# A fused attention, gated-MLP and residual kernel: LayerNorm of chunk 1 brought forward, its loads and spreads put in another order

## The chip, the core and the metric

The kernel runs on one core of one Trainium2 chip. The metric is the device time of one execution in microseconds (us); it is given as the median of several executions. The profile is of one further execution. Its span runs from its first to its last instruction and is a little shorter than that execution's device time.

## What is computed

One transformer block without the second normalization: x is normalized over its 640 columns (2048 rows, bfloat16), and both a sliding-window attention (32 heads of 20, window 256) and a gated MLP (640 to 1536 to 640) read the normalized rows. Both results are added to x.

```python
xn = _layernorm(x, axis=-1)
return x + _A_ref(xn, A_wqkv, A_wo) + _B_ref(xn, B_w_gate, B_w_up, B_w_down)

# _A_ref
qkv = (x @ wqkv).reshape(B, S, 3, H, Dh).transpose(2, 0, 3, 1, 4)
scores = einsum("bhqd,bhkd->bhqk", q, k) * (Dh ** -0.5)
scores = where(mask, scores, -1e9)      # 0 <= i - j < 256
o = einsum("bhqk,bhkd->bhqd", softmax(scores), v)
return o.transpose(0, 2, 1, 3).reshape(B, S, D) @ wo

# _B_ref
h = sigmoid(x @ w_gate) * (x @ w_up)
return h @ w_down
```

## The kernel before the change

**Chunks and units.** The 2048 rows are worked in four chunks (c = 0 to 3) of 512 rows. For each chunk there are Q and K (`g_qk`, five blocks each of five matmuls), V (`g_v`, four units), gate and up (`g_gu`: for each of twelve blocks f a gate half, five matmuls, then an up half, five matmuls), and the output (`g_out`: the down projection and the attention projection into the same sums). The attention runs in steps t (four for each pair of heads pr in chunk 0, five in later chunks): `scores` fills one large PSUM tile `ps` (L492), ACT takes its exponential (L498), POOL and DVE mask it (L481, L509). Two steps after the end of a pair, `pv` multiplies by V (L525).

**What sets the order on TensorE.** PE executes in program order. The main loop (L740) issues a step's scores, then pulls other units from the list of `fill` by hand-written costs: 1080 for a gate half, an up half, a Q block or a K block, 1360 for a V unit. A step pulls at least 1800, and more by a running credit. Generators in `mix` let a second generator advance between the units without any cost, so LayerNorm work of a later chunk is issued between them. Before the change the list is: gate and up of chunk 0 for f = 0 to 9, x of chunk 2, the turning of wo, Q and K of chunk 1, V of chunk 1, the loads of the down weights wd and of wo, gate and up for f = 10 and 11, and so on. Six halves are pulled before step 0.

**LayerNorm of a later chunk.** DVE makes statistics (L214, L220), POOL the reciprocal root (L228, L229), DVE the normalized rows (L233) and a 32 x 32 transpose (L250). `turn_rows` then writes the rows to DRAM in one DMA (L255) and reads them back in four (L257) as xnT, the operand of every projection of that chunk. Before the change, `g_quick(1)` does all of it between the gate and up halves of chunk 0.

**Q and K to heads.** `proj_block` puts a block's sum (L272) into a tile `st` of six buffers, by DVE for Q (L276) and by ACT for K (L278), and a DMA writes it to a DRAM scratch (L280). `spread` reads the scratch back with the heads on the partitions the scores want (L290), one DMA for each r = 0 to 3 of q and of k; head pair pr uses r = pr. The scratch's rows beyond 20 of each 32 are zeroed once (`clear`, L153). Both chunks use the same scratch, so a store of chunk 1 may only run when the spreads of chunk 0 have read it.

**Queues.** All of these DMAs are issued by SP (SyncE), in program order. An issue that waits holds back all that follow on it.

**Softmax scaling.** `finish_pair` transposes the accumulators on DVE and appends `scale_pair` and `turn_pair` (both DVE work) to `fill.behind`; `Fill.one` (L577) pops one of them after each unit that has a cost.

**PSUM.** Sums of all units share four one-bank buffers (`ps_d`), taken in turn; `ps` of the scores is one buffer of four banks, so the scores of a step wait for the exponential of the step before it.

Of the kernel before, what the change touches and what calls it, by code (L numbers as in the profile page):

```python
# [9 lines left out]
P = 128  # L10
# [56 lines left out]
def kernel(  # L67
# [42 lines left out]
    def load_x(c):  # L110
        t = xp.tile([P, SBC, D], BF16, name="xc")
        xc[c] = t
        rows = x2[c * CW:(c + 1) * CW, :].rearrange("(a n t) d -> a t n d", a=SBC, n=SBC)
        for a in range(SBC):
            nc.sync.dma_start(out=t[32 * a:32 * a + 32], in_=rows[a])
# [35 lines left out]
    def clear(w):  # L151
        rows = scratch[w].rearrange("(h j) s -> h (j s)", j=32)[:, DH * CW:]
        nc.sync.dma_start(out=rows.rearrange("h (a e) -> h a e", a=4), in_=zero[:, 0:3, :])  # L153

    def load_gu(t, w, k, lo=0, hi=FS):
        nc.sync.dma_start(out=t[k][:, :, lo:hi],
                          in_=w.rearrange("(c p) f -> p c f", p=P)[:, :, k * FS + lo:k * FS + hi])

    load_gu(wg, B_w_gate, 0, 0, FS // 2)
    load_gu(wu, B_w_up, 0, 0, FS // 2)  # L160
    clear("q")
    clear("k")
    load_gu(wg, B_w_gate, 0, FS // 2)

    def load_rest():
        load_gu(wg, B_w_gate, 1, 0, FS // 2)
        load_gu(wu, B_w_up, 1, 0, FS // 2)
        load_gu(wg, B_w_gate, 1, FS // 2)
        load_gu(wu, B_w_up, 1, FS // 2)
        spread("q", 0, 2, NP)  # L170
        spread("k", 0, 2, NP)

    def load_wd():
        wd_r = B_w_down.rearrange("(c p) d -> p c d", p=P)
        for lo, hi in ((0, 3), (3, 6), (6, 8), (8, 10), (10, FC)):
            nc.sync.dma_start(out=wd[:, lo:hi, :], in_=wd_r[:, lo:hi, :])
# [67 lines left out]
    def turn_block(c, s):  # L244

        if s == 0:
            turns[c] = lnp.tile([P, SBC * D], BF16, name="turn", bufs=1)
        out_v = turns[c].rearrange("p (g m n t) -> p n g m t", g=HG, m=DC, n=SBC)
        in_v = xc[c][:, s, :].rearrange("p (m g j) -> p g m j", g=HG, m=DC)
        nc.vector.transpose(out=out_v[:, s], in_=in_v)  # L250

    def turn_rows(c):
        xnT[c] = xtp.tile([P, SBC, DC, P], BF16, name="xnT")
        rows = tc.dram_tile([HG, P, D], BF16, name=f"turn{c}")
        nc.sync.dma_start(out=rows.rearrange("g p e -> p g e"), in_=turns[c].rearrange("p (g e) -> p g e", g=HG))  # L255
        for g in range(HG):
            nc.sync.dma_start(out=xnT[c][32 * g:32 * g + 32].rearrange("p a m t -> p a (m t)"),  # L257
                              in_=rows[g].rearrange("(a j) e -> j a e", j=32))
# [20 lines left out]
        dst = scratch[w].rearrange("(h j) s -> h j s", j=32)  # L279
        nc.sync.dma_start(out=dst[:, 4 * m:4 * m + 4, :], in_=st)  # L280

    def spread(w, c, r0, r1):

        half, first = divmod(r0, NP // 2)
        if first == 0:
            qk[w, c, half] = (qp if w == "q" else kp).tile([P, GH, CW], BF16, name=w + "T")
        src = scratch[w].rearrange("(a r p) s -> p r a s", a=2, p=P)
        to = qk[w, c, half].rearrange("p (r a) s -> p r a s", a=2)
        for r in range(r0, r1):
            nc.sync.dma_start(out=to[:, r % 2], in_=src[:, r])  # L290

    def new_v(c, s):
        v = vp.tile([P, 2, 16 * VW + 11], BF16, name="v")
# [37 lines left out]
    def g_stats(c, out):  # L331


        mvs = lnp.tile([P, SBC, nc.vector.BN_AGGR_DIM], FP32, name="mvs", bufs=1)
        for s in range(SBC):
            ln_block(c, s, mvs[:, s, :])
            if s == SBC - 1:
                rstds = rstd_blocks(mvs)
            yield 0
        yield 0  # L340
        out.extend((mvs, rstds))

    def norm_rows(c, s, mvs, rstds):
        norm_block(c, s, mvs[:, s, :], rstds[:, s:s + 1], xc[c][:, s, :])
# [10 lines left out]
                turn_rows(c)  # L355
            yield 0

    def g_quick(c):
        got = []
        yield from g_stats(c, got)  # L360
        for s in range(0, SBC, 2):
            norm_rows(c, s, *got)
            norm_rows(c, s + 1, *got)
            yield 0
        for s in range(SBC):
            turn_block(c, s)
            if s == SBC - 1:
                turn_rows(c)
            yield 0

    def g_qk(c):
        for w in "qk":
            for m in range(DC):
                proj_block(w, c, m)
                if c == 0 and w == "q" and m == 1:
                    load_x(1)
                yield 5 * MM
        if c:
            spread("q", c, 0, 2)
            spread("k", c, 0, 2)  # L380
        else:
            for r in range(2):
                spread("q", c, r, r + 1)
                spread("k", c, r, r + 1)
                if r == 0:
                    load_gu(wu, B_w_up, 0, FS // 2)
# [18 lines left out]
    def g_gu(c, f0, f1):  # L405
        for f in range(f0, f1):
            pg = ps_d.tile([P, CW], FP32, name="pg", tag="d")
            for d in range(DC):
                nc.tensor.matmul(pg, lhsT=part(wg, d, f), rhs=xnT[c][:, :, d, :],  # L409
                                 start=(d == 0), stop=(d == DC - 1))  # L410
            th = tp.tile([P, CW], FP32, name="th")
            nc.scalar.activation(out=th, in_=pg, func=TANH, scale=0.5)  # L412
            yield 5 * MM
            pu = ps_d.tile([P, CW], FP32, name="pu", tag="d")
            for d in range(DC):
                nc.tensor.matmul(pu, lhsT=part(wu, d, f), rhs=xnT[c][:, :, d, :],  # L416
                                 start=(d == 0), stop=(d == DC - 1))
            h = hp.tile([P, CW], BF16, name="h")
            ht[c, f] = h
            nc.vector.scalar_tensor_tensor(out=h, in0=th, scalar=1.0, in1=pu, op0=ADD, op1=MULT)  # L420
            yield 5 * MM
# [32 lines left out]
    def outp(c, s, ys, rows):  # L454
        for y, cut in zip(ys, HALVES):
            add_wo(c, s, y, cut)
        for y, cut in zip(ys, HALVES):
            add_x(y, cut, rows)
        store(c, s, rows)

    def g_out(c, between, ahead=()):
        coming = new_rows(c, 0)
        for s in range(SBC):
            rows = coming
            if s < SBC - 1:
                coming = new_rows(c, s + 1)
            if s == 0:
                yield from ahead
            ys = [ps_d.tile([P, CW], FP32, name=f"y{i}", tag="d") for i in range(2)]
            for y, cut in zip(ys, HALVES):  # L470
                yield from down(c, s, y, cut)
            if s == 0:
                yield from between
            outp(c, s, ys, rows)
            yield 10 * 136

# [85 lines left out]
    class Fill:  # L562
        def __init__(self):
            self.parts = []
            self.behind = []
            self.done = set()
            self.shut = set()

# [8 lines left out]
        def one(self):  # L577
            label, gen, _ = self.parts[0]
            try:
                cost = next(gen)  # L580
                if cost and self.behind:
                    self.behind.pop(0)()
                self.parts[0][2] -= cost
                return cost
            except StopIteration:
                self.parts.pop(0)
                self.done.add(label)
                return 0
# [14 lines left out]
    def mix(a, b, first, every=1, rest=True):  # L603

        for k, cost in enumerate(a):
            yield cost
            if k >= first and (k - first) % every == 0:
                yield next(b, 0)
        if rest:
            yield from b  # L610
# [77 lines left out]
    nc.scalar.activation(out=scr, in_=neghalf[:, 0:1], func=EXP)  # L688
    banks.close()
    ps_s = banks.enter_context(tc.tile_pool(name="ps_s", bufs=1, space=bass.MemoryType.PSUM))  # L690
    for _ in g_qk(0):
        pass
    load_rest()

    fill = Fill()
    GU = 10 * MM
# [2 lines left out]
    def later(load, *args):  # L699
        load(*args)  # L700
        yield 0

    norms1 = g_quick(1)
    norms2 = itertools.chain(g_norms(2, True), later(load_x, 3))
    norms3 = g_norms(3, False)
    fill.add("gu0a", mix(g_gu(0, 0, 4), norms1, 0, 1, False), 4 * GU)
    fill.add("gu0b", mix(g_gu(0, 4, 10), norms1, 0), 6 * GU)
    fill.add("x2", later(load_x, 2), 0)
    fill.add("wo_i", later(turn_wo), 0)
    fill.add("qk1", g_qk(1), 50 * MM)  # L710
    fill.add("v1", mix(g_v(1), norms2, 2, 1, False), 40 * 136)
    fill.add("wd", later(load_wd), 0)
    fill.add("wo", later(load_wo), 0)
    fill.add("gu0c", mix(g_gu(0, 10, 12), norms2, 0, 1, False), 2 * GU)
    fill.add("gu1a", mix(g_gu(1, 0, 2), norms2, 0, 1, False), 2 * GU)
    fill.add("out0", mix(g_out(0, g_gu(1, 2, 3)), norms2, 1, 1), OUT + GU)
    fill.add("qk2", mix(g_qk(2), norms3, 2, 1, False), 50 * MM)
# [108 lines left out]
```

## Time and profile before

| | us |
|---|---|
| median of 3 runs | 310.68 (310.26 to 310.72) |
| profiled execution, device time | 311.1 |
| its span | 309.4 |
| DVE, ACT, POOL busy | 187.2, 192.6, 79.1 |
| PE, all gate, up, Q/K matmul groups (L409, L416, L272) | 59.8, 59.8, 45.8 |
| DVE normalizing and transposing chunk 1 | 32.37 to 39.2 |
| turned rows of chunk 1: write issued, read back issued | 39.31, 45.52 to 48.62 |
| down weights: five loads issued | 71.17 to 75.79 |

The granted clock of TensorE is 1.00 throughout. PE is the engine to watch: idle time of the others costs only where PE waits for them. Times "at" a moment count from the start of the span. A column in square brackets of a timeline line gives the idle time of the engine before the line, and what ended it. The issue line of a DMA is not its transfer: it says when SP handed it over.

### The profile page before, as it was taken

What the parts mean: (1) busy time and instruction counts of PE and PEld (TensorE: products, weight loads), DVE (VectorE), ACT (ScalarE), POOL (GpSimd) and SP (SyncE); (2) the same over time, 40 slices, a digit from 0 to 9 for tenths busy, and PEclk for the clock granted to TensorE, in tenths of its full rate; (3) what the DMA queues carried; (4) which work ended last, traced back from release to release, by engine and by line L of the source; (5) the groups of instructions that cost most, each with busy time, mean ns of one, the idle gap of its engine ahead of it and who ended that gap; (6) DMA issues with size and microseconds to landing.
All of it is one profiled execution on the core that took longest, in us unless ns stands there. A gap on an engine that the chain in (4) does not pass through costs nothing.

```text
span 309.4 us, 10124 instructions
## 1 busy us (share of the span) xinstructions
PE 303.5 (98%) x4431; PEld 168.0 (54%) x4431; DVE 187.2 (61%) x372; ACT 192.6 (62%) x184; POOL 79.1 (26%) x172
## 2 busy tenths in 40 slices
PE   7999998999999999999999999999999999999996
PEld 3654443565456655644556655653445665444775
DVE  4736858659894679667653657346383627474423
ACT  6923875797674566869574656877676466768100
POOL 5000423133423123521223132331313232231100
PEclk9999999999999999999999999999999999999999
DMA  7987967549916722540251212560000110000301
GB/s 212 364 292 214 334 214 209 172 131 287 289 45 178 168 91 90 176 135 0 89 127 49 61 58 88 152 218 2 2 2 2 58 53 23 2 2 2 87 22 64
DMA packets 36140, 36.86 MB, mean 119 GB/s; under 512 B 2944, under 2 KB 35840, under 8 KB 36096
## 3 DMA queue, kind: packets, MB, share of 16 engines
q1 hardware_dynamic: 35232, 35.45, 37.7%
q10 hardware_dynamic: 864, 0.77, 0.9%
q8 instruction: 34, 0.56, 0.8%
q14 instruction: 10, 0.08, 0.1%
HBM read 25.59 MB, written 11.44 MB: 120 GB/s over the span
## 4 chain that ended last, share of the span: by engine, by line
PE 86%; DMA 4%; DVE 4%; issue 2%; ACT 1%; POOL 1%; SPq 1%; POOLq 0%; DVEq 0%
PE y L430 16%; PE pqk L272 15%; PE pu L416 14%; PE pg L409 13%; PE ps L492 8%; PE y L437 7%; PE pv L323 6%; PE acc L525 5%; DMA turn<-turn 2%; PE pv L303 1%; DMA xc<-in_A_x_dram 1%; ACT pT L498 1%; DMA xnT<-turn 1%; DVE h L420 1%; DVE stats L214 1%
## 5 line engine op out<-in xcount | busy, mean ns | idle before, releaser
L498 ACT ACTIVATE pT<-ps 128x2048 bf16<-128x2048 f32 x76 | 141.1, 1856 | 64.5 <-PE ps L492 56.9
L481 POOL TENSOR_SCALAR_AFFINE_SELECT pT<-pT 64x256 bf16<-64x256 bf16 (+1 forms) x120 | 68.1, 567 | 177.4 <-ACT pT L498 127.6
L409 PE MATMUL pg<-xnT,wg 128*128 128x512 bf16 x240 | 59.8, 380 | 0.0
L416 PE MATMUL pu<-xnT,wu 128*128 128x512 bf16 x240 | 59.8, 380 | 0.0
L430 PE MATMUL y<-wd,h 128*128 128x320 bf16 (+2 forms) x396 | 56.8, 295 | 0.0
L420 DVE SCALAR_TENSOR_TENSOR h<-th,pu 128x512 bf16<-128x512 f32 x48 | 32.6, 679 | 36.9 <-PE pu L416 18.9
L272 PE MATMUL pqk<-xnT,wqkv 128*128 128x512 bf16 x200 | 45.8, 381 | 1.3 <-DMA xnT<-turn 1.3
L430 PEld LDWEIGHTS <-h 128*128 128x128 bf16 x396 | 36.7, 98 | 16.2 <-issue 2.5
L509 DVE TENSOR_TENSOR pT<-pT,keep 128x512 bf16<-128x512 bf16 (+1 forms) x76 | 35.4, 468 | 11.5 <-ACT pT L498 10.5
L412 ACT ACTIVATE th<-pg 128x512 f32<-128x512 f32 x48 | 28.6, 595 | 15.5 <-PE pg L409 15.1
L416 PEld LDWEIGHTS <-wu 128*128 128x128 bf16 x240 | 22.0, 98 | 27.4 <-issue 2.7
L409 PEld LDWEIGHTS <-wg 128*128 128x128 bf16 x240 | 21.9, 98 | 27.0 <-issue 2.9
L272 PEld LDWEIGHTS <-wqkv 128*128 128x128 bf16 x200 | 22.4, 119 | 20.9 <-issue 3.5
L492 PE MATMUL ps<-qT,kT 20*64 20x320 bf16 (+4 forms) x1440 | 32.2, 260 | 0.1
L441 DVE SCALAR_TENSOR_TENSOR rows<-y,rows 128x320 bf16<-128x320 f32 x30 | 14.5, 490 | 27.0 <-PE y L437 24.6
L536 DVE STREAM_TRANSPOSE t<-acc 128x512 f32<-128x512 f32 x32 | 21.0, 695 | 13.6 <-PE acc L525 13.6
L492 PEld LDWEIGHTS <-kT 20*64 20x64 bf16 x1440 | 13.2, 103 | 23.4 <-issue 21.0
L437 PE MATMUL y<-wo,oc 128*128 128x320 bf16 (+2 forms) x165 | 24.2, 295 | 0.0
L525 PEld LDWEIGHTS <-v 64*32 64x32 bf16 x1440 | 17.1, 92 | 6.8 <-issue 1.8
L525 PE MATMUL acc<-pT,v 64*32 64x320 bf16 (+4 forms) x1440 | 20.3, 253 | 0.1
L437 PEld LDWEIGHTS <-oc 128*128 128x128 bf16 x165 | 15.6, 98 | 6.5 <-issue 0.8
L276 DVE CAST st<-pqk 128x512 bf16<-128x512 f32 x20 | 13.7, 686 | 7.4 <-PE pqk L272 7.2
(56 smaller groups left out, 173.6 us busy)
## 6 DMA issues: line engine op xcount, KB each, us to landing
qT<-sq SPq DMA_DIRECT2D x16, 256.0 KB, 4.5
kT<-sk SPq DMA_DIRECT2D x16, 256.0 KB, 4.8
xc<-in_A_x_dram SPq DMA_DIRECT2D x16, 160.0 KB, 4.2
sq<-st SPq DMA_DIRECT2D x20, 128.0 KB, 2.3
sk<-st SPq DMA_DIRECT2D x20, 128.0 KB, 2.1
out_dram<-rows SPq DMA_DIRECT2D x15, 160.0 KB, 1.8
wg<-in_B_w_gate_dram SPq DMA_DIRECT2D x4, 480.0 KB, 8.1
wu<-in_B_w_up_dram SPq DMA_DIRECT2D x4, 480.0 KB, 7.5
```

Of the source, the lines that this page charges most:

```text
L272: nc.tensor.matmul(ps, lhsT=wt[:, m, :], rhs=xnT[c][:, :, d, :], start=(d == 0), stop=(d == DC - 1))
L409: nc.tensor.matmul(pg, lhsT=part(wg, d, f), rhs=xnT[c][:, :, d, :], start=(d == 0), stop=(d == DC - 1))
L412: nc.scalar.activation(out=th, in_=pg, func=TANH, scale=0.5)
L416: nc.tensor.matmul(pu, lhsT=part(wu, d, f), rhs=xnT[c][:, :, d, :], start=(d == 0), stop=(d == DC - 1))
L420: nc.vector.scalar_tensor_tensor(out=h, in0=th, scalar=1.0, in1=pu, op0=ADD, op1=MULT)
L430: nc.tensor.matmul(y[:, 0:cut[1] - cut[0]], lhsT=ht[c, f][:, s * P:(s + 1) * P], rhs=wd[:, f, cut[0]:cut[1]], start=(f == 0), stop=False)
L437: nc.tensor.matmul(y[:, 0:cut[1] - cut[0]], lhsT=oc[c, m][:, s * P:(s + 1) * P], rhs=wo[:, m, cut[0]:cut[1]], start=False, stop=(m == DC - 1))
L481: nc.gpsimd.affine_select(out=part, in_=part, pattern=pattern, compare_op=GE, fill=0.0, base=-1 if sign > 0 else 0, channel_multiplier=sign)
L492: nc.tensor.matmul(ps[side * U:(side + 1) * U, i, col * U:(col + n) * U], lhsT=qk["k", kc, half][32 * i:32 * i + DH, 2 * r + side, kb * U: ...
L498: nc.scalar.activation(out=pt[:, :, 0:used, :], in_=ps[:, :, 0:used * U], func=EXP, scale=SCALE)
L509: nc.vector.tensor_tensor(out=part, in0=part, in1=limit.to_broadcast([P, HG, n * U]), op=MIN)
L525: nc.tensor.matmul(accs[side][32 * i:32 * i + 32, q * U:(q + n) * U], lhsT=vt[sb][rows, b, at:at + 32], rhs=pt[rows, i, col:col + n, :], s ...
```

## The change

1. Ahead of chunk 0's Q and K, SP issues the load of x of chunk 1 and the second half of the first gate weights. The two clears go behind the store of q block 2 and of k block 0.
2. The statistics of chunk 1 are issued behind K blocks 0 to 3 and the reciprocal roots behind the last of them. `g_first` issues the normalizing and the transposes behind the first six halves of gate and up, and `turn_rows(1)` ahead of the seventh.
3. Gate and up of chunk 0 are cut into f = 0 to 5, 6 to 8 and 9 to 11 instead of 0 to 3, 4 to 9, 10 and 11, so Q and K of chunk 1 come two halves earlier.
4. The spreads r = 2 and 3 of chunk 0 go from SP, ahead of the turned rows, to POOL, between the halves of f = 6 to 8 (`g_late`). The last of them is followed by a memset of one element of wd on DVE and the five loads of wd on SP; they no longer come behind V of chunk 1.
5. x of chunk 2, the second halves of the second gate and up weights and the turning of wo go behind q block 0, q block 2 and k block 0 of chunk 1.
6. `fill.hold` keeps `scale_pair` and `turn_pair` from being popped behind a gate half; `g_out` flushes what is left ahead of the first output sum.

```diff
-    clear("q")
-    clear("k")
-    load_gu(wg, B_w_gate, 0, FS // 2)
-
-    def load_rest():
-        load_gu(wg, B_w_gate, 1, 0, FS // 2)
-        load_gu(wu, B_w_up, 1, 0, FS // 2)
+    def load_second():
         load_gu(wg, B_w_gate, 1, FS // 2)
         load_gu(wu, B_w_up, 1, FS // 2)
-        spread("q", 0, 2, NP)
-        spread("k", 0, 2, NP)
...
-    def spread(w, c, r0, r1):
+    def spread(w, c, r0, r1, queue=nc.sync):
...
-            nc.sync.dma_start(out=to[:, r % 2], in_=src[:, r])
+            queue.dma_start(out=to[:, r % 2], in_=src[:, r])
...
-    def g_quick(c):
-        got = []
-        yield from g_stats(c, got)
+    mvs1 = lnp.tile([P, SBC, nc.vector.BN_AGGR_DIM], FP32, name="mvs1", bufs=1)
+
+    def g_first(rstds):
         for s in range(0, SBC, 2):
-            norm_rows(c, s, *got)
-            norm_rows(c, s + 1, *got)
+            norm_rows(1, s, mvs1, rstds)
+            norm_rows(1, s + 1, mvs1, rstds)
             yield 0
         for s in range(SBC):
-            turn_block(c, s)
+            turn_block(1, s)
             if s == SBC - 1:
-                turn_rows(c)
+                turn_rows(1)
             yield 0
 
-    def g_qk(c):
+    def g_late():
+        for r in range(2, NP):
+            for w in "qk":
+                spread(w, 0, r, r + 1, nc.gpsimd)
+                if (r, w) == (NP - 1, "k"):
+                    nc.vector.memset(wd[:, 0, 0:1], 0.0)
+                    load_wd()
+                yield 0
+
+    def g_qk(c, behind={}):
         for w in "qk":
             for m in range(DC):
                 proj_block(w, c, m)
-                if c == 0 and w == "q" and m == 1:
-                    load_x(1)
+                behind.get((w, m), lambda: None)()
                 yield 5 * MM
...
             nc.scalar.activation(out=th, in_=pg, func=TANH, scale=0.5)
+            fill.hold = True
             yield 5 * MM
+            fill.hold = False
             pu = ps_d.tile([P, CW], FP32, name="pu", tag="d")
...
                 yield from between
+                fill.flush()
             outp(c, s, ys, rows)
...
-                if cost and self.behind:
+                if cost and self.behind and not self.hold:
                     self.behind.pop(0)()
...
-    for _ in g_qk(0):
-        pass
-    load_rest()
+    load_x(1)
+    load_gu(wg, B_w_gate, 0, FS // 2)
+    for k, _ in enumerate(g_qk(0, {("q", 2): lambda: clear("q"), ("k", 0): lambda: clear("k")})):
+        if DC <= k < DC + SBC:
+            ln_block(1, k - DC, mvs1[:, k - DC, :])
+            if k == DC + SBC - 1:
+                rstds1 = rstd_blocks(mvs1)
+    load_gu(wg, B_w_gate, 1, 0, FS // 2)
+    load_gu(wu, B_w_up, 1, 0, FS // 2)
...
-    norms1 = g_quick(1)
...
-    fill.add("gu0a", mix(g_gu(0, 0, 4), norms1, 0, 1, False), 4 * GU)
-    fill.add("gu0b", mix(g_gu(0, 4, 10), norms1, 0), 6 * GU)
-    fill.add("x2", later(load_x, 2), 0)
-    fill.add("wo_i", later(turn_wo), 0)
-    fill.add("qk1", g_qk(1), 50 * MM)
+    fill.add("gu0a", mix(g_gu(0, 0, 6), g_first(rstds1), 0), 6 * GU)
+    fill.add("gu0b", mix(g_gu(0, 6, 9), g_late(), 1), 3 * GU)
+    fill.add("qk1", g_qk(1, {("q", 0): lambda: load_x(2), ("q", 2): load_second, ("k", 0): turn_wo}), 50 * MM)
     fill.add("v1", mix(g_v(1), norms2, 2, 1, False), 40 * 136)
-    fill.add("wd", later(load_wd), 0)
     fill.add("wo", later(load_wo), 0)
-    fill.add("gu0c", mix(g_gu(0, 10, 12), norms2, 0, 1, False), 2 * GU)
+    fill.add("gu0c", mix(g_gu(0, 9, 12), norms2, 0, 1, False), 3 * GU)
```

## The prediction

> **What bounds the kernel.** I read the page first, for the busy shares, then the PE timeline for holes, then SP, DVE and ACT around the hole.
>
> ```profile
> span 309.4 us, 10124 instructions
> ...
> PE 303.5 (98%) x4431; PEld 168.0 (54%) x4431; DVE 187.2 (61%) x372; ACT 192.6 (62%) x184; POOL 79.1 (26%) x172
> ```
>
> PE is busy 98% and executes in program order, so only its holes can be won: 309.4 - 303.5 = 5.9 us, with head and tail. The timeline shows the largest one (columns: start, duration, engine, line, operation, tiles, count; in brackets the idle time before and its releaser):
>
> ```profile
> 45.71 0.43 PE L492 MATMUL ps<-qT,kT 20*64 20x64 bf16 x24
> 46.07 1.25 PE L416 MATMUL pu<-xnT,wu 128*128 128x512 bf16 x5
> 47.16 1.24 PE L409 MATMUL pg<-xnT,wg 128*128 128x512 bf16 x5
> 48.33 0.42 PE L492 MATMUL ps<-qT,kT 20*64 20x320 bf16 x16
> 48.69 1.25 PE L416 MATMUL pu<-xnT,wu 128*128 128x512 bf16 x5
> ...
> 51.27 2.33 PE L272 MATMUL pqk<-xnT,wqkv 128*128 128x512 bf16 x10 [1.33 <-DMA xnT<-turn]
> ```
>
> A half takes PE 1.08 from start to start. The Q blocks of chunk 1 could have begun at 48.69 + 1.08 = 49.77 and began at 51.27: **1.50 us** lost to the turned rows. SP shows why they are late:
>
> ```profile
> 39.31 0.36 SPq L255 DMA_DIRECT2D turn<-turn  x1
> 45.52 3.10 SPq L257 DMA_DIRECT2D xnT<-turn  x4
> 48.66 1.85 SPq L115 DMA_DIRECT2D xc<-in_A_x_dram  x4
> ```
>
> From the write's issue to the read's it is 6.2; then 5.7 more until PE starts. A second, smaller hole stands ahead of pair (0, 3):
>
> ```profile
> 82.72 0.10 PEld L525 LDWEIGHTS <-v 64*32 64x32 bf16 x4 [0.42 <-ACT pT L498]
> ...
> 83.11 0.88 PEld L525 LDWEIGHTS <-v 64*32 64x32 bf16 x68 [0.29 <-DVE h L420]
> ```
>
> There PE waits 0.3 to 0.4 for a PSUM buffer that DVE's h (82.37 to 83.05) frees late.
>
> **The change, part by part.**
>
> *Loads and clears in Q and K: nothing.* x of chunk 1 (0.66 MB) and the gate half (0.49 MB) change places with the clears (0.79 MB); the bytes to 25 us are the same. DMA is full to about 18 us and moves 253 GB/s in 18 to 21, against 383 in 8 to 11, so the clears fit there. If that cover went, the spread r = 0 would be late for step 0 at 30.62, us for us.
>
> *Statistics: nothing.* DVE's last Q cast ends at 19.55; then it idles 3.35 us until the statistics at 22.91. Four blocks take 4 x 1.1 = 4.4: done by 24. POOL's two operations take 1.3 (0.23 + 1.04), so the norms, new ahead of the first h on DVE, start near 25.4 and end at 26.3; that h could start at 26.4. The rest (0.93 of norms, four transposes of 0.8) lies between the h's and ends near 32.4, beside PE. The cover: each h must be done three units later; 0.5 to 1 us of delay per h leaves more than 1.
>
> *Turned rows: -1.50.* The write is issued near 32.5 instead of 39.31. Ahead in the queue are two weight quarters, issued at 29.1 and 29.6 as before; 0.98 MB after the r = 1 spreads end near 35.5. A later write of this kind, alone, needs 3.86 (92.73 to 96.59); 35.5 + 3.9 + 5.7 = 45.1. The first Q block now stands where the half at 47.16 stood: two us of margin, and POOL's first spread costs at most 0.26 MB / 286 GB/s = 0.9 of it.
>
> *Spreads r = 2, 3 on POOL: nothing on PE.* No row shows a DMA issued by POOL. Bounds: 0.36 to 2.54 for an issue (SP's own, the longer with a full queue); landing at 4.5 to 4.8 (the spreads of the page). On POOL, q2 comes behind the mask of step 2 (ends 40.5), k2 and q3 behind that of step 4 (45.9), k3 behind that of step 5 (49.7). They delay a mask by one or two issues, under 3 us; its pair is read two steps (5 us) later. Pair 2 needs q2 and k2 at step 8, now near 54.6: at 2.5 per issue, 45.9 + 2.5 + 4.8 = 53.2. I take 1 us per issue, nearer to SP's median of 0.5 than to the full queue.
>
> *Down weights early, and what stands behind them: +0.9.* The memset follows the transposes that end at 47.16 on DVE (0.2, by the aggregate of 0.21); one h is queued behind it. SP then issues wd from 47.3. Behind it on SP now stand, in this order: store q0, x (four), q1, q2, two weight halves, q3, q4, k0, eight wo turns, k1 to k4, and the spreads. In the old order x and the wo turns alone were ahead. The transfers run in order of issue, and K's copies need them: `st` has six buffers, so k2's copy (ACT) waits for the store of q1, and k4's for q3. The pulls charge a half, a Q and a K block alike, so the steps keep their places among the units. At 1.08 per unit, 0.36 per step and 0.96 per pair PE's new order is Q from 47.16, step 7 at 51.9, step 8 at 54.6, k1 and k2 from 54.9, pair 1 at 57.1, step 9 at 58.1, k3 and k4 from 58.4, step 10 at 60.7, V, step 11 at 63.9. Ahead of a step stand a copy and the exponential:
>
> ```profile
> 58.87 0.59 ACT L278 CAST st<-pqk 128x512 bf16<-128x512 f32 x1 [0.37 <-DMA sq<-st]
> 60.23 1.88 ACT L498 ACTIVATE pT<-ps 128x2048 bf16<-128x2048 f32 x1 [0.77 <-PE ps L492]
> ```
>
> That is 0.59 + 1.88 + 0.1 = 2.55, so PE loses L(q1) - 58.1 or L(q3) - 61.3, whichever is more, with L a landing. The transfer rates (last column):
>
> ```profile
> 33.00:38.00 5.00, 5.00 (x61) 2.00 (x60) 5.00 (x10) 3.80 (x5) 1.99 (x4) 1.00 1.09 332
> 69.00:74.00 5.00, 5.00 (x139) 3.45 (x136) 3.94 (x9) 3.46 (x4) 1.33 (x6) 1.00 0.93 286
> 76.00:81.00 5.00, 5.00 (x53) 2.04 (x52) 4.93 (x12) 4.17 (x5) 1.76 (x5) 1.00 1.07 371
> ```
>
> They are weight halves, spreads with other traffic, and mostly wd. From a first packet at 48.3: wd 1.97 MB at 371 = 5.3; what is left of POOL's spreads, 0.52 MB at 332 = 1.6; q0 0.4; x 0.66 at 371 = 1.8; q1 0.4: 57.8, landed 58.4. Then q2 0.4, weights 0.98 at 332 = 3.0, q3 0.4: 61.6, landed 62.2. PE loses 0.3 or **0.9**. Bounds: all of it, 4.13 MB, at 371 with the spreads already done, 48.3 + 11.1 + 0.6 = 60.0: nothing; all with 0.79 MB of spreads at 286, 66.1: 4.8. Most of the traffic is wd, x and weights, so I stay near 371 and 332.
>
> By the Trainium skill, "DMA: Bandwidth & Descriptors", section "Issuing engines are not separate DMA queues", what POOL issues runs on the same 16 DMA engines and interleaves. No run shows it yet; without sharing the loss would be nothing (62.2 - 1.6 = 60.6).
>
> *Wd, wo, spreads of chunk 1: nothing.* Wd was loaded at 71 to 81 for a use at 84.4 and now lands by 56. The wo turns are issued near 59 to 64, k4's store near 67, the spreads near 69 (68.2 before) for step 16 at 80.1: eight us of margin.
>
> *Scaling behind an up sum: -0.4.* DVE's h goes ahead of 1.6 to 2 us of scaling. With the three halves f = 9 to 11 late, the normalizing of chunk 2 also runs two units earlier, so the h in question ends near 81, ahead of the pair. Bounds: 0 and 0.4, plus 0.15 ahead of step 19, which I leave out. Elsewhere no h holds PE up.
>
> **Sum:** -1.5 - 0.4 + 0.9 = **-1.0**: the profiled 311.1 (span 309.4) would be 310.1 (308.4). The median stands 0.4 under that execution: 310.68 - 1.0 = **309.7**.
>
> **Rivals.**
>
> *No wait at K (0.20).* All of -1.9: 308.8. For it: the rates above, 371 with everything moving. Against it: 4.1 MB must pass in 13 us.
>
> *The wait takes the hole's place (0.20).* At some 310 GB/s on average q3 lands at 63.2, the loss is 1.9 and the time 310.7. For it: 286 where stores and spreads are mixed. Against it: those stretches also have gaps between issues.
>
> *Q's stores wait for POOL (0.17), the slower side.* The store q0 on SP must wait until POOL's spread q3 has read the scratch. If POOL cannot issue while DVE works, then:
>
> ```profile
> 46.00:52.00 6.00, 4.67 (x51) 1.92 (x36) 5.36 (x9) 4.24 (x3) 2.46 (x4) 1.00 0.69 188
> ```
>
> DVE is busy 5.36 of these 6 us. q3 would be issued near 51.7 and land at 51.7 + 4.5 = 56.2. The queue has then run dry; from 57.3, 0.4 + 1.8 + 0.8 + 3.0 + 0.4 gives 63.7, landed 64.3: a loss of 3.0, net +1.1: 311.8. It decides from a q3 landing at about 55. Against it: POOL's masks do run in this stretch. The Trainium skill, "SBUF — State Buffer", section of the "DVE blocks DMA" trap, has this rule: descriptors of POOL's DMAs cannot be written while DVE is in a two-port mode. No run shows it here.
>
> *The change doesn't do it (0.05).* The rows still come after 49: 310.7. Only if the write took over 7 us, against 6.2 before with 1 MB of spreads ahead.
>
> **How the numbers follow.** The forecast has 0.38; the parts run 309.1 to 310.4. To tell from no change takes 0.2%, 0.62: under 310.06 or over 311.3. Faster: 0.32 of the forecast and the 0.20 without a wait, 0.52. Same: 0.06, 0.20, 0.04 of the last, making 0.30. Slower: the POOL case and a mishap of the last, 0.18. The range, 308.6 to 311.7, leaves out the lower part of the case without a wait (0.08) and the upper half of the POOL case with the mishaps of the last (0.10).
>
> **What would show it.** Right: no idle PE ahead of the first L272 of chunk 1; xnT's read issued before 40; ACT's L278 idle behind `sq<-st` near 58 and 61.5, and PE idle at steps 10 and 11 by as much. Wrong: a PE wait for xnT, kT or qT in 24 to 56, a q0 store issued after 55, a PE hole near 83 as before, or a PE hole in the first 30 us.

## The result, and the profile after

| | before | after |
|---|---|---|
| median, us | 310.55 (310.26 to 310.72) | 313.59 (313.17 to 314.87) |
| profiled execution, its span | 311.1, 309.4 | 313.36, 311.6 |
| again, in a second comparison | 311.30 (310.68 to 313.12) | 313.99 (313.01 to 315.02) |

The change makes the kernel slower: ratio 1.0106 (95% interval 1.0074 to 1.0137), and 1.0089 (1.0067 to 1.0110) in the second comparison. The two profiled executions are 2.26 us apart, and the terms below are counted between them. The medians are 3.04 apart; the 0.8 between the two differences is within what single executions differ by in their first 30 us (last section). Medians here are over all executions; in the table of the experiments, the ratio of wd_late leaves out its three slow ones of ten (315.6 to 316.6).

The page of the kernel after, with busy time and share of the span, and the one DMA queue that the page of before does not have:

```profile
span 311.6 us, 10139 instructions
...
PE 303.3 (97%) x4431; PEld 168.3 (54%) x4431; DVE 186.3 (60%) x373; ACT 192.6 (62%) x184; POOL 82.1 (26%) x176
...
q0 software_dynamic: 320, 1.05, 1.1%
```

PE does the same 4431 matmuls in the same 303 us. So the 2.2 us of span are again idle time of PE, and its timeline shows where (columns as in the prediction):

```profile
46.23 1.25 PE L419 MATMUL pu<-xnT,wu 128*128 128x512 bf16 x5
47.32 1.24 PE L265 MATMUL pqk<-xnT,wqkv 128*128 128x512 bf16 x5
...
58.40 0.43 PE L496 MATMUL ps<-qT,kT 20*64 20x64 bf16 x24
60.06 2.32 PE L265 MATMUL pqk<-xnT,wqkv 128*128 128x512 bf16 x10 [1.24 <-ACT st L271]
64.04 0.42 PE L496 MATMUL ps<-qT,kT 20*64 20x320 bf16 x16 [1.66 <-ACT pT L502]
64.40 2.91 PE L316 MATMUL pv<-wqkv,xnT 128*64 128x320 bf16 x40
67.73 0.37 PE L496 MATMUL ps<-qT,kT 20*64 20x128 bf16 x16 [0.42 <-ACT pT L502]
...
83.70 1.24 PE L419 MATMUL pu<-xnT,wu 128*128 128x512 bf16 x5
84.87 1.03 PE L529 MATMUL acc<-pT,v 64*32 64x320 bf16 x72
```

At 47.32 the first Q block of chunk 1 follows the up half without a bracket: the hole that the turned rows made is gone. At 84.87 pair (0, 3) follows without one too. But between step 9 (58.40) and step 12 (70.86) stand three new holes, in the K blocks of chunk 1 and at steps 10 and 11. Without a wait this stretch takes 8.97 us (67.14 - 58.17 in the run q_in_turn with the spreads on SP, below); here it takes 12.46. That is **3.49 us lost**, where 0.9 was predicted.

The ACT timeline names the wait. The copies on L271 move a K block from PSUM to the staging tile `st`:

```profile
54.91 0.58 ACT L271 CAST st<-pqk 128x512 bf16<-128x512 f32 x1 [0.74 <-PE pqk L265]
55.39 1.88 ACT L502 ACTIVATE pT<-ps 128x2048 bf16<-128x2048 f32 x1
59.43 0.58 ACT L271 CAST st<-pqk 128x512 bf16<-128x512 f32 x1 [2.15 <-DMA sq<-st]
61.63 0.58 ACT L271 CAST st<-pqk 128x512 bf16<-128x512 f32 x1 [1.62 <-DMA sq<-st]
62.11 1.88 ACT L502 ACTIVATE pT<-ps 128x2048 bf16<-128x2048 f32 x1
...
65.31 0.58 ACT L271 CAST st<-pqk 128x512 bf16<-128x512 f32 x1 [0.84 <-PE pv L316]
```

The second, third and fifth K copy wait for the first, second and fourth store of Q, which still read the `st` buffers (the one behind the fifth is shown by its landing, below). The exponential at 62.11 stands behind the copy at 61.63, and step 10 on PE behind the exponential. The bracket of the last line names PE, but a copy of a K block does not read the V block that it names. The store q3, whose buffer it needs, landed at 65.21, 0.1 ahead of it: the bracket names the releaser that came last by the profile.

SP's issues in its timeline:

```profile
32.73 0.37 SPq L248 DMA_DIRECT2D turn<-turn  x1
38.20 1.75 SPq L250 DMA_DIRECT2D xnT<-turn  x4
47.38 3.58 SPq L169 DMA_DIRECT2D wd<-in_B_w_down_dram  x5
51.13 0.78 SPq L273 DMA_DIRECT2D sq<-st  x1
51.96 2.48 SPq L115 DMA_DIRECT2D xc<-in_A_x_dram  x4
55.00 3.10 SPq L273 DMA_DIRECT2D sq<-st  x2
59.03 0.39 SPq L156 DMA_DIRECT2D wg<-in_B_w_gate_dram  x1
59.46 0.56 SPq L156 DMA_DIRECT2D wu<-in_B_w_up_dram  x1
60.52 1.17 SPq L273 DMA_DIRECT2D sq<-st  x2
```

The waits of the same queue between 54 and 62 (us in total, times, longest):

```profile
SPq L273 <- DMA wd<-in_B_w_down_dram: 2.5, 2, 2.0
SPq L156 <- DMA wd<-in_B_w_down_dram: 0.9, 1, 0.9
```

A store of Q has nothing to do with wd, and yet its issue waits for it. The semaphore records of the trace show why. Each landing stands there as 16 increments of a semaphore; the table gives the first, the median (the ninth) and the last of them, and the semaphore that they went to:

```
            issue   sem  first  median  last
wd 1        47.38   109  50.83  51.22   52.76
wd 2        47.82   101  52.22  52.60   54.11
wd 3        48.35   102  53.14  53.49   54.94
wd 4        48.89   103  54.27  54.95   57.50
wd 5        50.46   104  55.81  56.49   59.01
q0          51.13   106  56.16  57.02   59.33
x 1         51.96   107  57.01  57.78   59.83
x 4         54.12   101  59.30  59.85   61.18
q1          55.00   102  59.52  60.25   61.47
q2          57.58   103  59.72  60.49   61.80
gate half   59.03   104  62.24  62.73   63.53
up half     59.46   106  63.81  64.23   64.84
q3          60.52   107  64.13  64.49   65.21
```

Two things are to be seen. SP's DMAs go round eight semaphores (101 to 104 and 106 to 109), so an issue waits until the DMA eight before has landed: q2 is issued at 57.58 behind wd 4 (57.50), the gate half at 59.03 behind wd 5 (59.01). And a landing is the last of sixteen: from wd 4 to q0 the last increment comes 2.3 to 2.6 us behind the median one, the last but one 2.0 to 2.3, and the other fourteen at most 1.1.

### The profile page after: what moved, and what is told of

The parts are those of the page before. It is cut to its first block, busy times and chain, and to the rows that moved or that the text cites. A ratio compares the mean times of both kernels' runs of the same rounds, so it can differ in the third digit from the quotient of the medians.

```text
span 311.6 us, 10139 instructions
## 1 busy us (share of the span) xinstructions
PE 303.3 (97%) x4431; PEld 168.3 (54%) x4431; DVE 186.3 (60%) x373; ACT 192.6 (62%) x184; POOL 82.1 (26%) x176
## 4 chain that ended last, share of the span: by engine, by line
PE 89%; DMA 6%; ACT 2%; SPq 1%; DVE 1%; issue 0%; ACTq 0%
PE y L433 17%; PE pu L419 17%; PE pg L410 17%; PE pqk L265 11%; PE ps L496 8%; PE y L440 7%; PE acc L529 6%; PE pv L316 5%; DMA wd<-in_B_w_down_dram 2%; DMA sq<-st 2%; ACT pT L502 2%; DMA wqkv<-in_A_wqkv_dram 2%; PE pv L296 1%; PE pvh L296 0%; DVE t L540 0%
## 5 line engine op out<-in xcount | busy, mean ns | idle before, releaser
L271 ACT CAST st<-pqk 128x512 bf16<-128x512 f32 x20 | 11.1, 593 | 13.0 <-PE pqk L265 6.2
```

## The experiments

Every kernel below is the kernel after with the edit shown; times are medians, ratios are against before on the same chip.

| run | us | before, us | ratio (95%) |
|---|---|---|---|
| q_in_turn | 309.89 | 311.07 | 0.9967 (0.9946 to 0.9989) |
| spread_sp | 311.64 | 311.07 | 1.0016 (0.9986 to 1.0045) |
| wd_late | 312.57 | 311.07 | 1.0021 (0.9996 to 1.0047) |
| wd_pool | 316.18 | 311.07 | 1.0161 (1.0122 to 1.0199) |
| after_again | 313.99 | 311.30 | 1.0089 (1.0067 to 1.0110) |
| x_behind | 311.09 | 311.30 | 0.9992 (0.9970 to 1.0015) |
| qt_sp | 309.48 | 311.30 | 0.9946 (0.9927 to 0.9965) |
| qt_no_hold | 312.16, one execution | 311.30 | |
| x_wide | 312.71, one execution | 311.32 | |
| xb_sp | 310.26 | 311.32 | 0.9956 (0.9933 to 0.9978) |
| qt_xb_sp | 309.22 | 311.32 | 0.9939 (0.9926 to 0.9952) |

**Is it the staging tile? q_in_turn** gives the Q blocks of chunk 1 a place of their own, so that no K copy needs a buffer that a Q store reads.

```diff
-        st = stp.tile([P, CW], BF16, name="st")
+        if c == 1 and w == "q":
+            if m == 0:
+                turns["st"] = lnp.tile([P, SBC * D], BF16, name="turn", bufs=1)
+            st = turns["st"][:, m * CW:(m + 1) * CW]
+        else:
+            st = stp.tile([P, CW], BF16, name="st")
```

> After the change, with one thing taken away: the five Q blocks of chunk 1 are staged in the 5 KB tile of the turned rows, which is idle then, and K alone in the six st buffers, so no K copy can wait for a Q store. Staging theory (ACT's K copies wait for late Q stores, and the scores for the exponential behind them): ACT idles under 0.3 us behind the Q stores, the PE holes ahead of steps 9 to 12 (1.45, 1.83 and 0.59 us by starts) shrink to under 0.4 in all, and the time falls by 3 to 3.7 us to 309.9 to 310.6 or, if nothing else was lost, under 309.5. Rival (POOL's masks or the PSUM buffers hold the scores up, and the store wait only falls on the same place): holes of over 2 us stay and the time is over 312.

The ACT timeline of q_in_turn, the same copies (now L276, in pairs):

```profile
56.23 0.59 ACT L276 CAST st<-pqk 128x512 bf16<-128x512 f32 x1 [0.74 <-PE pqk L265]
56.71 1.88 ACT L507 ACTIVATE pT<-ps 128x2048 bf16<-128x2048 f32 x1
58.48 1.08 ACT L276 CAST st<-pqk 128x512 bf16<-128x512 f32 x2
60.23 1.88 ACT L507 ACTIVATE pT<-ps 128x2048 bf16<-128x2048 f32 x1 [0.67 <-PE ps L501]
62.01 1.07 ACT L276 CAST st<-pqk 128x512 bf16<-128x512 f32 x2
```

No copy waits for a store, though the stores land even later than in the kernel after (q0 59.13, q1 63.16, q3 66.24). Steps 9 to 12 take 8.97. From step 0 to step 75 the kernel takes 251.75 us, against 253.51 before: 1.76 gained, and the kernel after takes 255.25. So the whole loss inside the loop is the wait of the K copies for `st`. The median is 309.89, as expected.

**Is it POOL? spread_sp** issues the spreads r = 2 and 3 on SP.

```diff
-                spread(w, 0, r, r + 1, nc.gpsimd)
+                spread(w, 0, r, r + 1)
```

> After the change, with the spreads r = 2 and 3 at the same places but issued by SP. Staging theory: SP has nothing else then, so they are issued near 40 to 47 and move before the down weights; the weights, the stores and the copies come about 1 us earlier, the holes shrink from 3.9 to 2.5 to 3.2 us, time 312.4 to 313.2. Rival (POOL's DMAs are what makes the stores late): the holes go, time under 310.8.

Its ACT timeline:

```profile
60.51 0.59 ACT L271 CAST st<-pqk 128x512 bf16<-128x512 f32 x1 [3.01 <-DMA sq<-st]
60.99 1.88 ACT L502 ACTIVATE pT<-ps 128x2048 bf16<-128x2048 f32 x1
```

The wait is there still, now mostly for one store (q1: median 58.44, last 60.41), and steps 9 to 12 take 12.79, so 3.8 are lost in the profiled execution. That is more than expected, but this execution is the slowest of ten (310.60 to 313.21). The median, 311.64, lies under the expected range: it is 0.57 above before, where the kernel after is 2.7 and 3.0 above in its two comparisons. So the wait does not need DMAs on POOL, but they make it longer: by 1.8 to 2.1 us, by an estimate from these medians less the 0.36 that follows. No trace shows the wait in a typical execution of spread_sp.

The 0.36 lie at the other end: from the start of the last matmul to the end of the span spread_sp takes 2.89, as before, where the kernel after takes 3.25. The four kernels with the spreads on SP show 2.88 to 2.90; the kernel after and the six others with them on POOL show 3.24 to 3.26, but wd_pool, with the most DMAs on POOL, shows 3.01. The semaphore rows at the end of the trace say why. SP waits there for its DMA semaphores one after another, in a fixed order with 109 last, and each wait takes 0.06. The semaphores go round with each DMA that SP and ACT issue: 168 in before and spread_sp, 164 in the kernel after, 159 in wd_pool. So the last store of the output has 109, 104 or 108, and when it lands (2.04 to 2.10 behind the start of the last matmul) none, four or one of the waits are still to come. The four waits are 0.25 of the 0.36; the rest is a landing 0.04 later and 0.07 in what SP and POOL do behind the waits. So the 0.36 follow from the place of the last store's semaphore, not from POOL as such.

**Is it wd ahead of the stores? wd_late** loads wd behind V of chunk 1 again.

```diff
                 spread(w, 0, r, r + 1, nc.gpsimd)
-                if (r, w) == (NP - 1, "k"):
-                    nc.vector.memset(wd[:, 0, 0:1], 0.0)
-                    load_wd()
...
     fill.add("v1", mix(g_v(1), norms2, 2, 1, False), 40 * 136)
+    fill.add("wd", later(load_wd), 0)
```

> After the change, with the down weights back behind V of chunk 1, without the memset. Staging theory with the queue's order as the cause of the late stores: store q0 lands near 54 instead of 59.3, q1 near 57, so the K copies wait under 0.7 us in all, the holes shrink to under 1 us and the time is 309.3 to 310.6. Rival (x of chunk 2 and the two weight halves alone are enough to make the stores late): q1 and q3 still land over 2 us after their copies are due, time over 311.5. A new risk, the same in both: the weights land near 83 to 85 and are wanted near 84.

The stores land at 53.92 (q0), 57.54 (q1) and 62.59 (q3). One K copy still waits 0.98, for q3, and steps 9 to 12 take 9.40: 0.43 lost, under 1 us as expected. But the time is 312.57, not 309.3 to 310.6: the gain is lost at the other end, by the risk that was named. Its PE timeline shows it:

```profile
83.70 1.56 PE L430 MATMUL y<-wd,h 128*128 128x320 bf16 x9
86.88 1.25 PE L430 MATMUL y<-wd,h 128*128 128x320 bf16 x8 [1.62 <-DMA wd<-in_B_w_down_dram]
```

Behind V, wd stands behind the spreads of chunk 1. Its first load is issued at 73.77 (before: 71.17), the last lands at 86.84 (84.91), and the sums that read it begin at 83.70 (84.41): PE waits 1.62. In the new order the old place is too late in this execution.

**Is it the order in SP's queue? wd_pool** lets POOL issue the five loads of wd, so that the stores are not behind them.

```diff
-            nc.sync.dma_start(out=wd[:, lo:hi, :], in_=wd_r[:, lo:hi, :])
+            nc.gpsimd.dma_start(out=wd[:, lo:hi, :], in_=wd_r[:, lo:hi, :])
```

> After the change, with the same five loads of the down weights at the same place, issued by POOL instead of SP. Order in SP's queue as the cause: the Q stores no longer stand behind 2 MB, they share the engines with it; q0 lands 2 us or more earlier, the holes shrink by at least 1.5 us and the time is 310.5 to 312. Rival (bandwidth as the cause, whichever queue): the stores land as late as now or later, since POOL's packets are larger, holes of 3 us and more, time 313 to 315.

Its ACT timeline:

```profile
63.63 0.59 ACT L271 CAST st<-pqk 128x512 bf16<-128x512 f32 x1 [6.29 <-DMA sq<-st]
```

The store q0 lands at 54.97, 4.4 us earlier than in the kernel after: in this the theory of the queue's order holds. But the store q1 is issued at 53.19, earlier than the 55.00 of the kernel after, and lands at 63.48, later than its 61.47. Steps 9 to 12 take 15.23, so 6.3 are lost, and the time is 316.18, above both ranges. What decides is the shared bandwidth. The packets of POOL's loads have 5120 bytes in the records, SP's of the same loads 1280, and while both move SP's come slowly: x's second load is issued at 51.64 and lands at 59.13. Taking wd out of the queue does not take it out of the way.

**How far does the first comparison repeat? after_again** is the kernel after, unchanged.

> The changed kernel itself beside the kernel before and the next three on one chip. From the first comparison: 1.006 to 1.013 of the time before; three holes of 3.4 us together ahead of steps 9 to 12 behind ACT's wait for the Q stores.

PE waits 0.46 ahead of the K blocks and 2.50 ahead of step 10, and not ahead of step 11; steps 9 to 12 take 12.08, so 3.1 are lost. Steps 0 to 75 take 255.32 (255.25 in the first), because 0.47 more are lost behind step 0, where an up half waits for its weights.

**Is it x of chunk 2? x_behind** moves its four loads behind k block 0, so behind all stores of Q.

```diff
-    fill.add("qk1", g_qk(1, {("q", 0): lambda: load_x(2), ("q", 2): load_second, ("k", 0): turn_wo}), 50 * MM)
+    fill.add("qk1", g_qk(1, {("q", 2): load_second, ("k", 0): lambda: (load_x(2), turn_wo())}), 50 * MM)
```

> The changed kernel with x of chunk 2 loaded behind k block 0 instead of q block 0. If x's four loads (0.66 MB to 32 partitions each, about 216 GB/s) are what makes q1's and q3's stores late: q1 lands near 58.5 and q3 near 62.5, the holes shrink from 3.4 to about 1 us, the time falls by 2 to 2.5 us against the changed kernel. If the down weights ahead are the cause: q0 and q1 move by under 1 us and holes of over 2 us stay.

2.9 us come off the median of after_again. In the profiled execution q1 lands at 57.61 and q3 at 61.48, ACT waits 0.18 and 0.41 for them, and PE does not wait in steps 9 to 12. Not all of it need be x's place in the queue: q0, which stands ahead of x in both kernels, lands at 57.26, against 59.33 and 58.58 in the two executions of the kernel after. In these executions wd or x alone ahead of the stores costs 0.43 at most, and both together 3.1 to 3.5; xb_sp below shows that x's place alone is not a safe cure. What is left against before is the slower end (3.24) and 0.37 behind step 0, ahead of an up half.

**Is it that x moves slowly? x_wide** loads x of chunk 2 in four DMAs of 128 partitions rather than 32, in one execution. Its rows come in another order, so this kernel serves for timing only.

```diff
+        if c == 2:
+            for n in range(SBC):
+                nc.sync.dma_start(out=t[:, n, :], in_=xr[:, c * SBC + n, :])
+            return
```

> The changed kernel, but x of chunk 2 is loaded by four DMAs of 128 partitions each instead of 32 (same place, bytes, packets of 1280 B; the rows of chunk 2 then stand in another order, so its outputs are those of other rows). If x is slow because each of its DMAs writes 32 partitions (216 GB/s, packets of 104 ns): packets take 55 ns, q1 lands near 59.5 instead of 61.5 and q3 near 63 instead of 65, the holes of steps 9 to 12 shrink from 3.4 to 1.5 to 2.5 us. If the rate comes from the mixture in the queue: 104 ns and the same holes.

Its ACT timeline:

```profile
58.61 0.59 ACT L275 CAST st<-pqk 128x512 bf16<-128x512 f32 x1 [1.72 <-DMA sq<-st]
60.68 0.58 ACT L275 CAST st<-pqk 128x512 bf16<-128x512 f32 x1 [1.48 <-DMA sq<-st]
...
64.64 0.59 ACT L275 CAST st<-pqk 128x512 bf16<-128x512 f32 x1 [1.12 <-DMA sq<-st]
```

A packet of x takes 55 ns instead of 104, as expected, but steps 9 to 12 take 12.18, between the 12.46 and 12.08 of the kernel after: no gain is shown. q1 is now issued at 56.56, behind the landing of wd 3 (56.50, its median at 53.68), and lands at 60.52. The slow rate is real, but in this execution the wait for the landing eight back and the last of the sixteen increments take its place.

**Is the hold needed? qt_no_hold** is q_in_turn without it, in one execution.

```diff
-            fill.hold = True
```

> Q staged in the tile of the turned rows, without the hold: scaling may again come ahead of h. If the hold closes the old hole ahead of pair (0, 3) (0.38 us): a hole of 0.2 to 0.5 us is there again near 84, step 0 to 75 takes 252.0 to 252.3 us. Rival (the earlier normalizing of chunk 2 closes it alone): no hole, 251.7 us.

Its PE timeline:

```profile
80.32 0.34 PE L500 MATMUL ps<-qT,kT 20*64 20x320 bf16 x8 [0.17 <-DMA kT<-sk]
...
82.85 1.03 PE L533 MATMUL acc<-pT,v 64*32 64x320 bf16 x72
...
157.61 1.67 PE L437 MATMUL y<-wd,h 128*128 128x320 bf16 x11 [0.51 <-DVE h L427]
```

Ahead of pair (0, 3) no wait comes back (82.85, no bracket): the h ends at 81.01 without the hold too, as the earlier normalizing of chunk 2 would have it. The hold pays elsewhere: without it an output sum waits 0.51 for an h. Neither before nor the kernel after has a wait for h there. Steps 0 to 75 take 252.83, more than either expectation: against q_in_turn 0.37 are lost at step 16 and 0.69 at this sum, by the starts of the steps.

**Which combination is best? qt_sp** is q_in_turn with the spreads on SP, **xb_sp** is x_behind with them, **qt_xb_sp** has all three edits; the diffs are those above.

> Q of chunk 1 staged in the tile of the turned rows, and the spreads r = 2 and 3 issued by SP instead of POOL. Staging theory: no hole in steps 9 to 12, step 0 to step 75 takes 251.7 us as with POOL's spreads (253.5 before). Tail theory (a kernel with DMAs on POOL ends 0.36 us later: 3.25 against 2.89 us from the last matmul to the end): the tail is 2.9 us and the time is 1.8 us under before, ratio near 0.994. Rival (the tail's difference is scatter): 3.2 us.

> The changed kernel with two placements altered: x of chunk 2 behind k block 0, and the spreads r = 2 and 3 on SP. Staging theory and tail theory together: no wait of K for the Q stores over 0.3 us, no hole in steps 9 to 12, a tail of 2.9 us; 1.8 us under before, ratio 0.994, as with Q staged elsewhere. Rival (the freed queue makes x late for the statistics of chunk 2, or the spreads of chunk 1 late for step 16): a hole of over 0.3 us after step 12.

> Q staged in the tile of the turned rows, x behind k block 0, spreads on SP. If nothing but the holes is left to win: the same 251.7 us from step 0 to 75 and ratio 0.994 to 0.995; the spread of k for chunk 1 is issued about 2 us earlier than with x behind q block 0.

qt_sp takes 251.86 from step 0 to 75 and 2.88 at the end. In xb_sp, against the expectation, the store q3 lands at 63.04 and a K copy waits for it (again the bracket names PE):

```profile
63.14 0.58 ACT L271 CAST st<-pqk 128x512 bf16<-128x512 f32 x1 [1.73 <-PE pv L316]
```

PE loses 1.2 by it. Ahead of q3 in the queue a gate half lands at 60.42, with its median at 58.00, and the up half at 62.83, with its median at 60.22: with `st` shared, a lag under the weights is enough. Five of its twelve executions took 309.2 to 309.6, so the loss does not come each time. In qt_xb_sp nothing is lost: steps 9 to 12 take 8.98, and step 0 to 75 takes 251.76.

It is the fastest of all, 2.1 us under before. That it beats qt_sp is not shown: 0.9939 and 0.9946 lie inside each other's intervals, and what x's later place should have given, the spreads of chunk 1 some two us earlier, did not come (71.49 against 71.69). What it gains over before from step 0 to 75, 1.75, is the hole of the turned rows and the one ahead of pair (0, 3); the staging keeps the waits of K from eating it up.

## Why the prediction was wrong

| term of the sum | predicted | measured |
|---|---|---|
| first 30 us (step 0) | 0 | +0.16 |
| turned rows (steps 0 to 7) | -1.50 | -1.48 |
| wd early, and what stands behind (steps 9 to 12) | +0.9 | +3.49 |
| scaling, pair (0, 3) | -0.4 | -0.38 |
| the rest to step 75 | 0 | +0.1 |
| from the last matmul's start to the end | not counted | +0.36 |
| sum | -1.0 | +2.25 |

**Down weights early, and what stands behind them** is the step that failed: the term was sized at +0.9 and measured +3.49. Its mechanism was right: the copies, the stores they wait for, and what PE loses are those named, and its formula holds. With step 9 at 58.40 instead of 58.1, L(q3) - 61.6 = 3.6 for the measured 3.49. One wait was not named, that of the second K copy for q0; it makes the hole in the K blocks, but adds nothing, because step 10 stands behind q1 in any case. The landings were wrong: 58.4 and 62.2 were predicted, 61.47 and 65.21 came.

For q1 the 3.1 us are made up so, by the medians of the table: the end of wd with POOL's last spread at 56.49 instead of 55.2 (+1.3; of these 0.8 because the first packet of wd moved at 49.1, not 48.3); x took 2.8 from q0's median to that of its fourth load, not 1.8 (+1.0: its packets of 1280 bytes took 104 ns, where those to 128 partitions took 55); a store 0.5 rather than 0.4 (+0.1); from the median to the last increment 1.2, not 0.6 (+0.6). For q3 come the issues held back by the landing eight before: between the medians of q2 and the up half lie 3.7 us, not 3.0.

So the transfers were taken too short in two ways. The first is the rate: 371 GB/s was taken for wd and x. The kernel after moved 336 GB/s in 50 to 53, and then, in the second row mostly x (window, its length, busy time and count of PE, PEld, DVE, ACT and POOL, the granted clock, the DMA share and GB/s):

```profile
53.00:56.00 3.00, 3.00 (x29) 1.47 (x28) 1.85 (x4) 2.25 (x3) 0.00 (x0) 1.00 1.02 343
56.00:59.00 3.00, 2.83 (x104) 1.81 (x102) 0.84 (x2) 1.27 (x1) 1.17 (x2) 1.00 1.12 254
```

The second is the landing: each term was sized at the mean rate of all sixteen engines, and a wait ends with the last. The prediction adds 0.6 from the end of a transfer to its landing without a row for it. By its terms q0 should have landed at 56.2; its median increment came at 57.0 and its last at 59.3. The Trainium skill says it in "DMA: Bandwidth & Descriptors", section "Why a DMA increments its semaphore by 16 and not by 1": the engines finish independently and only the full 16 mean that all data has landed. The trace agrees, by these 2.3 us. Of the 3.1 us at q1 the movement made 2.4 and this lag 0.6.

Why the last one or two of sixteen lag is open. The lag is seen in other runs at other loads (q1 of spread_sp, without a DMA on POOL, 2.0; wd 3 of x_wide 2.8). An instruction queue moves packets of 16 KB that take about 1 us each, in the kernel after at 46.34 (1.0) and 58.28 (1.3); that these are on the lagging engines could not be read from the trace, and no run tests it.

The upper bound written for this term, 4.8, holds the 3.49. The value taken stood near the fast rates because most bytes were of the fast kind. The range that followed was too narrow: of the rivals, *the wait takes the hole's place* named the right place with 1.9, still near half of what came. It came from a rate of some 310 GB/s for all; it had no lag either.

**Turned rows: -1.50** held, to 0.02. The write was issued at 32.73 (32.5), the read at 38.20 (before 40), the last of the rows landed at 42.97 (by the sum of the prediction PE could start at 45.1), and the first Q block stands at 47.32 (47.16).

**Scaling behind an up sum: -0.4** held in size. Of the two reasons given, qt_no_hold shows that the hold is not needed there; the h ends at 81.01 without it, near the 81 of the other reason.

**Spreads on POOL: nothing on PE.** Right inside the loop: an issue takes 0.72 to 0.94 (1 was taken), and no mask is late enough to hold a pair. The room that they take beside wd was counted in the term above. The 0.36 at the end were not counted.

**Q's stores wait for POOL**, the slower rival, did not decide: the store q0 was issued at 51.13, and the spread q3 had landed at 50.01. The trace has one row that seems to be in its favour. The POOL timeline of the kernel after, two of the issues:

```profile
46.71 0.72 POOL L283 DMA_DIRECT2D qT<-sq  x1
...
49.82 0.73 POOL L283 DMA_DIRECT2D kT<-sk  x1
```

And its window 50 to 53 (columns as above):

```profile
50.00:53.00 3.00, 3.00 (x30) 1.47 (x29) 3.00 (x7) 1.21 (x2) 1.54 (x3) 1.00 1.02 336
```

The spread k3, issued with DVE busy all of the next three us, landed after 6.7 us (56.53), the three before it after 3.2 to 3.3. That fits the rule of the "DVE blocks DMA" trap that the prediction cites from the Trainium skill, but wd was moving too. wd_late, with wd elsewhere, tells the two apart:

```profile
50.27 0.73 POOL L283 DMA_DIRECT2D kT<-sk  x1
```

```profile
50.00:53.00 3.00, 3.00 (x30) 1.47 (x29) 3.00 (x6) 1.37 (x1) 2.00 (x4) 1.00 0.33 102
```

DVE is busy for all three us again, and k3 lands after 3.1 us (53.35). So the 6.7 us come with wd's traffic, not with a busy DVE. Whether DVE was in a two-port mode in these three us the trace does not tell, so the rule itself is neither borne out nor refuted. The other rule that the prediction cites from the Trainium skill, that DMAs of all issuing engines share the sixteen engines, is borne out by wd_pool.

**Eight us of margin** for the spreads of chunk 1 was too much. The first kT spread was issued at 73.0, not near 69; the first two had landed at 76.8, and step 16 stands at 82.25. In qt_no_hold they were issued later yet (74.58), the last increment of the first came 3.0 us behind the median (80.27), and step 16 waited for it.

## What to carry to other kernels

A load that is moved earlier goes ahead of stores, and a store holds its staging buffer: count who waits for that buffer before the queue's room is given away, and give the staging its own place if it is short. Size a wait by the last of a DMA's sixteen increments in the trace, not by bytes over the best rate seen; the last stood 0.6 to 2.6 us behind the median here, and 254 GB/s came where 371 was taken. One profiled execution can be the slowest of its kind: hold it against the median before a cause is named. And a load taken off one queue still takes its bandwidth on the other.

## What the runs showed of the hardware

- A DMA issued on POOL moves packets of 4096 or 5120 bytes (four rows) where SP's have one row, 1280 for wd. With wd on POOL, SP's store q1 took 10.3 us from issue to landing (6.5 in the kernel after).
- The end of a kernel behind its last matmul took 2.88 to 2.90, 3.01 or 3.24 to 3.26 us, by the place of the last store's semaphore in SP's last row of waits (spread_sp above).
- The first 10 us are not the same in each execution. Here are the first V matmuls in the PE timeline of q_in_turn:

```profile
7.19 2.87 PE L301 MATMUL pv<-wqkv,xnT 128*128 128x320 bf16 x10
```

And in that of before:

```profile
7.03 1.60 PE L303 MATMUL pv<-wqkv,xnT 128*128 128x320 bf16 x10
```

The same ten matmuls took 1.27 us longer, with a granted clock shown as 1.00; why is open. Step 0 stood at 32.11 in that execution and at 30.79 in the kernel after. Of ten executions of q_in_turn, six took 309.56 to 309.91 and four 311.31 to 311.36, the profiled one among the four; whether the other three began so too is not known. So its span of 309.5 hides what its steps 0 to 75 show.
